# Twenty far units of a sliding-window attention backward turned by DMA instead of TensorE, with smaller K and V rings and gradient sums in four parts

## The chip, the cores and the metric

The kernel runs on one core of one Trainium2 chip. The metric is device time in microseconds (us) of one execution; several executions are timed, and one further execution is recorded by the hardware profiler. Engines are called as in the profile: PE is TensorE (PEld its weight loads), DVE is VectorE, ACT is ScalarE, POOL is GpSimd, SP is SyncE, which here only issues DMAs.

## The reference, cut to what matters

The reference is the forward and the backward of a gated mix of two branches for 2048 tokens of width 512: sliding-window attention (32 heads of 16, window 256) and a gated feed-forward network of width 1376. It returns the output and seven gradients (x, wqkv, wo, W_gate, W_up, W_down, gate_w).

```python
g = sigmoid((x * gate_w).sum(-1, keepdims=True))
a = attention(x, wqkv, wo)          # scores * Dh**-0.5, 0 <= q - k < 256, softmax
b = glu(x, W_gate, W_up, W_down)    # relu(x @ W_gate) * (x @ W_up) @ W_down
out = g * a + (1 - g) * b
_out, _vjp = jax.vjp(_f, x, wqkv, wo, W_gate, W_up, W_down, gate_w)
_grads = _vjp(grad_out)
```

## The kernel before, in words

Tokens stand in 16 tiles of 128. The program has three stages, and within each the order of all instructions is written out by hand (`tc.manual_schedule`); each engine runs its own list in that order, and semaphores make it wait for data and for free buffers.

**Stage 1 (0 to about 250 us)** is the feed-forward network: gate, up, the gradient of h, and the weight gradients (L363 to L435). **Stage 3 (from about 705 us)** computes W_down's product, wo's gradient, the output and the gradient of x (L1014 on).

**Stage 2 (about 250 to 705 us) is attention, which the change touches.** It runs over four blocks `c` of eight heads. In each block it goes over 16 query tiles `j`; each meets the key tiles `kb` = j (role "d", the diagonal), j-1 (role "m") and j-2 (role "f", far: the window's last part). Each such pair of tiles is done in two halves of four heads (`HH`), and one half is a *unit*: six units per j, from j = 2 on, in the order m, f, d (first halves) and m, d, f (second halves); 360 units in all, 112 of them far. The loop over `n` in the last part of stage 2 does, at step n:

- `front` (L687, L696 to L701) of unit n: PE's scores ST, ACT's exp into `Pu`, and on POOL the mask of d and f units;
- `front_dp` (L710) of unit n-1: PE's dPT, the product of V and the output's gradient;
- `gradp` (L715) of unit n-2: DVE's `Pd` = `Pu` * dPT;
- `rowsum` (L724, L726) of unit n-4: eight small products of PE, two for each of four heads, into BA;
- `flip`: `Pu` and `Pd` are needed with keys and queries exchanged. For d units, and for all m units but four, both halves lie in one tile (PPd, PPm; rings of three), and one DMA transpose on SP (L743), issued when the second half's `Pd` is there, turns 16 blocks of 128x128 into `p2d` or `p2m` (rings of three). The far units have tiles of their own (`Pu`, `Pd`; rings of two) and are turned on PE with rowsum: eight transposes into PSUM (`pt`, L753) and a copy by ACT or DVE (L72, L74) into a P2f tile (ring of four);
- `cd_piece` (L541, L544): for each key tile, when its last query tile is through, PE multiplies the turned tiles into CD. The pieces of one key tile stand in a list, one or two of them per step.

Beside the units there is filler work for PE, which a count (`credit`) lets in: the projections of the next group of four tiles (`project_parts`: Q, dO, a DMA transpose of both into `rows` (L181), K, V, and `tr_kv`, which writes kv with two memsets of POOL, L187 and L188), with a `due` step by which they must be in; and the sums of the gradient of wqkv of the block before (`grad_parts`, L641: four parts of four pieces of four matmuls). K and V of a group are tiles K0, K1, V0, V1, KV1, in a pool of one buffer each (pjA) and one of two (pj), so that three groups can be there. Group g+1's K and V are made while group g runs, and group g's first two query tiles still read group g-1's.

SP's list holds, in one queue, the pair transposes (L743), `rows`, the spills of finished rows to DRAM (L564, 512 KB), the stores of gradient sums (L633), and early loads of stage 3's weights: `plan` says after which group's projections a weight may be turned (`turns`, L581) or loaded (`loads`, L606, L591) into a slot that projections no longer read (x0 to x3, d0 to d3, p0 to p3); `late` spaces them out. What does not fit there (`W_rest`) is issued at the end of attention and in stage 3.

Of the kernel before, what the change touches and what calls it, by code (L numbers as in the profile page):

```python
# [11 lines left out]
BF = mybir.dt.bfloat16  # L12
# [10 lines left out]
def kernel(  # L23
# [20 lines left out]
    nc = tc.nc  # L44
    P = 128
# [9 lines left out]
    NT = S // P  # L55
# [4 lines left out]
    NTG = S // TGW  # L60
    TPG = TGW // P
# [46 lines left out]
    pjA = ctx.enter_context(tc.tile_pool(name="pjA", bufs=1))  # L108
    pjs = {}
    pools = {}  # L110

    if True:
        HH = HG // 2
# [9 lines left out]
        def project_parts(c, tg):  # L123
            t4 = {}
            proj[(c, tg)] = t4
            pj = lambda: pjA if (c * NTG + tg) % 3 == 0 else pjs["b"]

            def mm(nm, which, eng):
                ps, tag, bufs, _, _ = pools["now"]
# [68 lines left out]
    with ExitStack() as p1, tc.manual_schedule():  # L198
# [43 lines left out]
        half = TPG // 2  # L242
# [270 lines left out]
    p3 = ctx  # L513
    if True:
        st = p3.enter_context(tc.tile_pool(name="attst", bufs=2))
        gwp = p3.enter_context(tc.tile_pool(name="gwp", bufs=2))
        p3b = ExitStack()
        pjs["b"] = p3b.enter_context(tc.tile_pool(name="pj", bufs=2))
        wk = p3b.enter_context(tc.tile_pool(name="attw", bufs=2))
        pps = ExitStack()  # L520
        ps = pps.enter_context(tc.tile_pool(name="attps", bufs=2, space=PSUM))
# [61 lines left out]
        def clear(name):  # L583
            nc.gpsimd.memset(W6[(name, FC - 1)][0:FC * P - F, :], 0.0)
# [32 lines left out]
        def load_gw():  # L617
# [2 lines left out]
        plan = {2: [load_gw], 5: turns("wqkv", A_wqkv, 0, 4, "p0"), 7: turns("wqkv", A_wqkv, 4, 8, "p1"),  # L620
                11: turns("wqkv", A_wqkv, 8, 12, "p2"),
                12: turns("Wg", B_W_gate, 0, 4, "x0") + turns("Wg", B_W_gate, 4, 8, "d0"),
                15: loads("Wd", B_W_down, 0, "x3") + loads("Wd", B_W_down, 4, "d3") + loads("Wd", B_W_down, 8, "p3")}
        W_rest = (turns("Wg", B_W_gate, 8, 12, "x1") + [lambda: clear("Wg")] + turns("Wu", B_W_up, 0, 4, "d1") + turns("Wu", B_W_up, 4, 8, "x2")
                  + turns("Wu", B_W_up, 8, 12, "d2") + [lambda: clear("Wu")])

        def grad_parts(c, tail=False):
            out = []
# [33 lines left out]
        for c in range(DC):  # L662
            for j in range(NT):
                kbs = [k for k in (j - 1, j, j - 2) if k >= 0]
                for half in range(2):
                    order = kbs if half or len(kbs) < 3 else [kbs[0], kbs[2], kbs[1]]
                    for ki, kb in enumerate(order):
                        u = Unit()
                        u.c, u.j, u.kb, u.half = c, j, kb, half
                        u.first = ki == 0 and half == 0  # L670
                        u.last = ki == len(kbs) - 1 and half == 1
                        u.role = ("d", "m", "f")[j - kb]
                        u.pair = u.role == "d" or (u.role == "m" and (c < DC - 1 or j < NT - 2))
                        u.own = u.role == "f"
                        u.dma = u.pair
                        units.append(u)
        NU = len(units)

# [2 lines left out]
        def front(u):  # L681
            tg, jl = u.j // TPG, u.j % TPG
            z = zt[(u.c * NTG + tg) % ZB]
            KTt = proj[(u.c, u.kb // TPG)][f"K{u.half}"]
            ksl = slice((u.kb % TPG) * P, (u.kb % TPG + 1) * P)
            ST = ps.tile([P, HH, P], F32, tag="M", bufs=4, name="ST")
            nc.tensor.matmul(ST[:], lhsT=KTt[:, ksl], rhs=z[:, 0, :, jl, :], start=True, stop=True)  # L687
            if not u.own:
                if u.half == 0:
                    tag = f"PP{u.role}"  # L690
                    pairs[(u.c, u.j, u.kb)] = wk.tile([P, 2, 2, HH, P], BF, tag=tag, bufs=3, name=tag)
                u.PP = pairs[(u.c, u.j, u.kb)][:, u.half, :, :, :]
                u.Pu, u.Pd = u.PP[:, 0, :, :], u.PP[:, 1, :, :]
            else:
                u.Pu = wk.tile([P, HH, P], BF, tag="Pu", bufs=2, name="Pu")
            nc.scalar.activation(u.Pu[:], ST[:], ACT.Exp)  # L696
            if u.role == "d":
                nc.gpsimd.affine_select(out=u.Pu[:], in_=u.Pu[:], compare_op=ALU.is_ge, fill=0.0, base=0,  # L698
                                        pattern=[[0, HH], [1, P]], channel_multiplier=-1)
            elif u.role == "f":  # L700
                nc.gpsimd.affine_select(out=u.Pu[:], in_=u.Pu[:], compare_op=ALU.is_ge, fill=0.0, base=-1,  # L701
                                        pattern=[[0, HH], [-1, P]], channel_multiplier=1)
# [7 lines left out]
            nc.tensor.matmul(u.dPT[:], lhsT=VTt[:, ksl], rhs=z[:, 1, :, jl, :], start=True, stop=True)  # L710

        def gradp(u):
            if u.own:
                u.Pd = wk.tile([P, HH, P], BF, tag="Pd", bufs=2, name="Pd")
            nc.vector.tensor_tensor(out=u.Pd[:], in0=u.Pu[:], in1=u.dPT[:], op=ALU.mult)  # L715

        def rowsum(u):
# [17 lines left out]
        def flip(u):  # L735
            key = (u.c, u.j, u.kb, "p2")
            if u.role != "f" and key not in P2 and not (u.pair and u.half == 0):
                P2[key] = wk.tile([P, 2, 2, HH, P], BF, tag=f"P2{u.role}", bufs=3, name=f"p2{u.role}")
            if u.dma:
                if u.pair and u.half == 0:  # L740
                    return
                hs = slice(0, 2) if u.pair else slice(u.half, u.half + 1)
                nc.sync.dma_start_transpose(out=P2[key][:, hs, :, :, :].rearrange("p b a h q -> p (b a h) q"),  # L743
                                            in_=pairs[(u.c, u.j, u.kb)][:, hs, :, :, :].rearrange("p b a h q -> p (b a h q)"))
                for b in range(2)[hs]:
                    P2[(u.c, u.j, u.kb, b)] = P2[key][:, b, :, :, :]
                return
            eng = ("act", "dve", "act")[copier["i"] % 3] if u.c == 0 else ("act", "dve")[copier["i"] % 2]
            copier["i"] += 1
            pt = psr.tile([P, 2, HH, P], BF, tag="TR", name="pt")  # L750
            for a, src in enumerate((u.Pu, u.Pd)):
                for hh in range(HH):
                    nc.tensor.transpose(pt[:, a, hh, :], src[:, hh, :], ident[:])  # L753
            p2 = P2[key][:, u.half, :, :, :] if u.role == "m" else wk.tile([P, 2, HH, P], BF, tag="P2f", bufs=4, name="p2")[:]
            evac(p2, pt[:], eng)
            P2[(u.c, u.j, u.kb, u.half)] = p2

# [81 lines left out]
        with tc.manual_schedule():  # L839
# [36 lines left out]
            while n <= NU + LAG or ev or cdq or bgq:  # L876
                now = ev.pop(n, [])
                u = units[n] if n < NU else None
                if u is not None:
                    gi = u.c * NTG + u.j // TPG  # L880
                    if u.first and u.j == 0:
                        sts[u.c] = st.tile([P, NT, 4, P], BF, tag="rows_st", name="rows_st")
                    if u.first and u.j % TPG == 0:
                        if gi + 1 < len(groups):
                            prq = project_parts(*groups[gi + 1]) if gi else second
                            due = n + sum(2 * min(3, j + 1) for j in range(u.j, u.j + TPG)) - 3
                            if gi + 2 == len(groups):
                                due -= 10
                    if u.first and u.j == TPG and ends:
                        copies.append(ends.pop(0))  # L890
                    if u.first and u.j == 1 and u.c > 0:
                        ready = grad_parts(u.c - 1)
                    if u.first and u.j == TPG - 1 and u.c > 0:
                        bgq += ready
                    front(u)
                    if u.last and gi + 1 == len(groups) and u.j % TPG in (1, 3):
                        ev.setdefault(n + 2, []).append(("dma", lambda i=(u.j % TPG) // 2: load_h(i)))
# [42 lines left out]
                if n >= NU:  # L940
                    if bgq:
                        held = background()
                    elif n > NU + 1:
                        for _ in range(2):
                            if len(S2["grads"]) > DC:
                                S2["grads"].pop(0)()
                elif held and credit > 0.3:
                    held = background()
                    credit -= 0.65
                elif prq and not held and ((credit > 0.4 and n > fed + 1) or due - n <= len(prq)):  # L950
                    fed = n
                    credit -= (0.44, 0.86, 0.86, 0.1, 0.86, 0.86)[len(prq) - 1]
                    prq.pop(0)()
                    if len(prq) == 4:
                        for k in range(NP):
                            ev.setdefault(n + 1 + k, []).append(("dve", lambda gi=gi, k=k: spread(gi + 1, k)))
                        ev.setdefault(n + 1, []).append(("dma", flush))
                    if not prq:
                        late += plan.get(gi + 1, [])
                elif bgq and len(prq) <= 2 and credit > 0.3:  # L960
                    held = background()
                    credit -= 0.65
                if u is not None and u.c == DC - 1 and not bgq and u.j > 6 and "grads" not in S2:
# [177 lines left out]
```

## Time and profile before

| | us |
|---|---|
| runs shown: median (lowest, highest) | 909.66 (908.64, 911.75) |
| the profiled execution | 907.26 |
| its span on the core | 905.5 |
| PE busy | 889.5 |
| DVE, POOL, ACT busy | 511.1, 492.8, 445.5 |

The granted TensorE clock was 1.00 throughout. The costliest groups of stage 2 are ST and dPT (360 matmuls each, 136 us of modelled duration each, about 0.215 us from start to start), the exps on ACT (360 of 0.60 us), the `gradp` products on DVE (360 of 0.68 us) and the masks on POOL (240 of 0.64 us). The flips on PE are 928 transposes (116 units), with 63 copies of 1.01 us on ACT and 53 of 0.69 us on DVE; the pair transposes by DMA are 64 for d and 58 for m, of 0.5 MB each.

How to read it: a matmul's duration in the trace is that of a pipelined instruction and overlaps the next one's, so what one costs PE is read from the starts. SP's rows (SPq) are the times that SP spends on issuing a DMA, not the transfer; a transfer's end is told by its landing. "DMA share" is the mean busy share of 16 DMA engines by the sum of packet times, and can exceed 1 where packets overlap.

### The profile page before, as it was taken

The numbers are of one execution on the slowest core, as the hardware profiler recorded it, in microseconds if no ns is written. First come the engines' busy times: TensorE is split into PE (matmuls) and PEld (weight loads), VectorE is DVE, ScalarE is ACT, GpSimd is POOL, SyncE is SP. The second block draws the span as 40 slices with busy tenths as digits, with TensorE's granted clock in tenths as the row PEclk, the third lists the DMA queues.
The fourth block names the chain that finished last, engine by engine and source line by source line (L and its number), as shares of the span: only waits on it lengthen the run. The fifth ranks groups of instructions, "written<-read, shape, count | busy, mean of one in ns | idle before, by whom it ended". The sixth has DMA issues, their size and how long they took to land.

```text
span 905.5 us, 25962 instructions
## 1 busy us (share of the span) xinstructions
PE 889.5 (98%) x10607; PEld 560.2 (62%) x10607; DVE 511.1 (56%) x946; ACT 445.5 (49%) x787; POOL 492.8 (54%) x937
## 2 busy tenths in 40 slices
PE   9999999999989999999999999999999999999998
PEld 5565655655657777677776677766677544444445
DVE  4433334434368887678886788877786101333343
ACT  6422232222278778667776677766787112111111
POOL 4544545545267778767777567876787100222232
PEclk9999999999999999999999999999999999999999
DMA  9998989999799999999999989999999899998940
GB/s 301 204 193 185 198 181 210 215 216 216 180 138 159 190 185 197 185 171 156 175 187 183 184 161 183 187 193 183 192 219 190 222 243 228 275 255 218 189 134 30
DMA packets 520984, 174.57 MB, mean 193 GB/s; under 512 B 446817, under 2 KB 519745, under 8 KB 520865
## 3 DMA queue, kind: packets, MB, share of 16 engines
q1 hardware_dynamic: 498624, 150.62, 89.6%
q10 hardware_dynamic: 20608, 17.70, 7.5%
q0 software_dynamic: 1632, 4.59, 1.5%
q8 instruction: 83, 1.36, 0.6%
q14 instruction: 37, 0.30, 0.1%
HBM read 34.37 MB, written 36.24 MB: 78 GB/s over the span
## 4 chain that ended last, share of the span: by engine, by line
PE 85%; DMA 4%; DVE 4%; ACT 2%; POOL 2%; SPq 2%; issue 1%; ACTq 0%; POOLq 0%; DVEq 0%
PE dxps L1068 8%; PE wps L412 8%; PE ST L687 7%; PE dPT L710 7%; PE pt L753 5%; PE dxps L1072 4%; PE dps L414 4%; PE pp L133 4%; PE dhps L363 4%; PE ups L363 4%; PE CD L541 4%; PE gps L363 4%; PE BA L724 4%; PE wps L641 4%; PE bps L1023 3%; PE BA L726 2%
## 5 line engine op out<-in xcount | busy, mean ns | idle before, releaser
L687 PE MATMUL ST<-z,K 128*128 128x512 bf16 x360 | 135.9, 378 | 3.3 <-ACT PPd L696 1.2
L710 PE MATMUL dPT<-z,V 128*128 128x512 bf16 x360 | 136.0, 378 | 1.8 <-DVE Pd L715 0.5
L698 POOL TENSOR_SCALAR_AFFINE_SELECT PPd<-PPd 128x512 bf16<-128x512 bf16 x128 | 81.3, 636 | 80.1 <-ACT PPd L696 80.0
L377 POOL TENSOR_TENSOR hT<-rg,upm 128x512 bf16<-128x512 bf16 x44 | 51.0, 1160 | 113.8 <-DVE upm L375 97.5
L412 PE MATMUL wps<-dgu_r,x_r 128*128 128x256 bf16 (+1 forms) x704 | 103.9, 270 | 0.0
L715 DVE TENSOR_TENSOR PPd<-PPd,dPT 128x512 bf16<-128x512 bf16 x128 | 86.9, 680 | 19.9 <-PE dPT L710 12.3
L701 POOL TENSOR_SCALAR_AFFINE_SELECT Pu<-Pu 128x512 bf16<-128x512 bf16 x112 | 72.0, 643 | 35.1 <-ACT Pu L696 34.0
L696 ACT ACTIVATE PPd<-ST 128x512 bf16<-128x512 f32 x128 | 77.0, 603 | 23.6 <-PE ST L687 18.8
L715 DVE TENSOR_TENSOR Pd<-Pu,dPT 128x512 bf16<-128x512 bf16 x112 | 76.4, 682 | 21.0 <-PE dPT L710 10.6
L412 PEld LDWEIGHTS <-x_r 128*128 128x128 bf16 x704 | 68.4, 98 | 30.9 <-issue 0.2
L696 ACT ACTIVATE Pu<-ST 128x512 bf16<-128x512 f32 x112 | 67.4, 602 | 37.2 <-PE ST L687 37.1
L715 DVE TENSOR_TENSOR PPm<-PPm,dPT 128x512 bf16<-128x512 bf16 x120 | 80.1, 667 | 7.1 <-PE dPT L710 6.1
L696 ACT ACTIVATE PPm<-ST 128x512 bf16<-128x512 f32 x120 | 72.5, 604 | 16.7 <-PE ST L687 16.2
L375 DVE SCALAR_TENSOR_TENSOR upm<-rg,ups 128x512 bf16<-128x512 bf16 x44 | 30.2, 685 | 81.8 <-ACT rg L369 43.1
L369 ACT ACTIVATE rg<-gps 128x512 bf16<-128x512 f32 x44 | 26.3, 597 | 89.0 <-PE gps L363 47.4
L414 PE MATMUL dps<-db_r,h_r 128*128 128x512 bf16 x176 | 66.8, 379 | 0.0
L1048 ACT COPY a_sb<-aps 128x512 f32<-128x512 f32 x16 | 9.4, 585 | 108.0 <-issue 99.8
L72 ACT COPY p<-pt 128x1024 bf16<-128x1024 bf16 x59 | 60.1, 1019 | 4.2
L387 POOL TENSOR_TENSOR dgu<-dh_sb,rg 128x512 bf16<-128x512 bf16 x44 | 58.0, 1318 | 5.3 <-ACT dh_sb L383 5.3
L386 DVE TENSOR_TENSOR dgu<-dh_sb,upm 128x512 bf16<-128x512 bf16 x44 | 34.5, 784 | 29.8 <-ACT dh_sb L383 26.1
L641 PE MATMUL wps<-rows_st,x_r 128*128 128x384 bf16 x256 | 50.3, 325 | 0.0
L133 PE MATMUL pp<-x,p 128*128 128x512 bf16 x192 | 49.0, 378 | 0.0
(178 smaller groups left out, 2323.2 us busy)
## 6 DMA issues: line engine op xcount, KB each, us to landing
dqkvo_d<-rows_st SPq DMA_DIRECT2D x15, 512.0 KB, 4.3
hT_d<-hT ACTq DMA_DIRECT2D x44, 128.0 KB, 2.5
dgT_d<-dgu ACTq DMA_DIRECT2D x44, 128.0 KB, 2.9
duT_d<-dgu ACTq DMA_DIRECT2D x44, 128.0 KB, 3.0
h<-hT_d SPq DMA_DIRECT2D x8, 640.0 KB, 4.9
dgT_g<-dgT_d SPq DMA_DIRECT2D x8, 640.0 KB, 5.2
duT_g<-duT_d SPq DMA_DIRECT2D x8, 640.0 KB, 6.5
go_g<-in_grad_out_dram SPq DMA_DIRECT2D x16, 256.0 KB, 4.7
```

Source lines behind the costliest of these rows:

```text
L133: nc.tensor.matmul(pp[:], lhsT=w_p[c][:, cd, which * P:(which + 1) * P], rhs=x_T[tg][:, cd, :], start=(cd == 0), stop=(cd == DC - 1))
L363: nc.tensor.matmul(out[:], lhsT=w(c), rhs=x(c), start=(c == 0), stop=(c == DC - 1))
L412: nc.tensor.matmul(acc["w"][:, c, 0:2 * nw], lhsT=x_r[:, t, c * P:(c + 1) * P], rhs=k.dgu_r[:, :, i, s0:P], start=(go_ and c % 2 == 0), st ...
L414: nc.tensor.matmul(acc["d"][:], lhsT=k.h_r[:, i, :], rhs=db_r[:, t, :], start=go_, stop=no_)
L641: nc.tensor.matmul(wps[:], lhsT=x_r[:, t, part * P:(part + 1) * P], rhs=sts[c][:, t, 0:3, :], start=first and t == t0, stop=last and t == ...
L687: nc.tensor.matmul(ST[:], lhsT=KTt[:, ksl], rhs=z[:, 0, :, jl, :], start=True, stop=True)
L696: nc.scalar.activation(u.Pu[:], ST[:], ACT.Exp)
L698: nc.gpsimd.affine_select(out=u.Pu[:], in_=u.Pu[:], compare_op=ALU.is_ge, fill=0.0, base=0, pattern=[[0, HH], [1, P]], channel_multiplier=-1)
L701: nc.gpsimd.affine_select(out=u.Pu[:], in_=u.Pu[:], compare_op=ALU.is_ge, fill=0.0, base=-1, pattern=[[0, HH], [-1, P]], channel_multiplier=1)
L710: nc.tensor.matmul(u.dPT[:], lhsT=VTt[:, ksl], rhs=z[:, 1, :, jl, :], start=True, stop=True)
L715: nc.vector.tensor_tensor(out=u.Pd[:], in0=u.Pu[:], in1=u.dPT[:], op=ALU.mult)
L1068: nc.tensor.matmul(to, lhsT=src[:, fc, lsl], rhs=W6[(wt, fc)][:, cols], start=(fc == 0 and wt == "Wg"), stop=False)
```

## The change

- In blocks 1, 2 and 3, 20 far units of the first half (j = 3, 4, 5, 6, 8, 9, 10, without 10 in block 3) are flipped by a DMA transpose of their own (eight blocks of 128x128), issued on SP three steps after the unit's front, instead of by PE.
- Every far unit has one tile for `Pu` and `Pd`: PFa (first halves, ring of three) or PFb (second halves, ring of one). P2f's ring grows from four to five.
- The pool pj has one buffer instead of two, and groups alternate between pjA and pj: K and V stand in rings of two. A `gate` holds back the K projection (and with it V and kv) until step 12 of the group (5 in a block's first group), when the older group's buffers come free; `due` of the last group is 6 instead of 10 steps early.
- The gradient sums of the block before are released in four parts, at j = 3, 5, 9 and 13, instead of all at j = 3, and may also run while the K projection waits at its gate.
- W_down is loaded into x1, d1 and x2 after groups 13 and 14 (it was x3, d3, p3 after group 15), and the weights of `W_rest` go into d2, x3, d3, p3.

```diff
--- before.py
+++ after.py
@@ -123,7 +123,7 @@
         def project_parts(c, tg):
             t4 = {}
             proj[(c, tg)] = t4
-            pj = lambda: pjA if (c * NTG + tg) % 3 == 0 else pjs["b"]
+            pj = lambda: pjA if (c * NTG + tg) % 2 == 0 else pjs["b"]
 
             def mm(nm, which, eng):
                 ps, tag, bufs, _, _ = pools["now"]
@@ -515,7 +515,7 @@
         st = p3.enter_context(tc.tile_pool(name="attst", bufs=2))
         gwp = p3.enter_context(tc.tile_pool(name="gwp", bufs=2))
         p3b = ExitStack()
-        pjs["b"] = p3b.enter_context(tc.tile_pool(name="pj", bufs=2))
+        pjs["b"] = p3b.enter_context(tc.tile_pool(name="pj", bufs=1))
         wk = p3b.enter_context(tc.tile_pool(name="attw", bufs=2))
         pps = ExitStack()
         ps = pps.enter_context(tc.tile_pool(name="attps", bufs=2, space=PSUM))
@@ -620,9 +620,9 @@
         plan = {2: [load_gw], 5: turns("wqkv", A_wqkv, 0, 4, "p0"), 7: turns("wqkv", A_wqkv, 4, 8, "p1"),
                 11: turns("wqkv", A_wqkv, 8, 12, "p2"),
                 12: turns("Wg", B_W_gate, 0, 4, "x0") + turns("Wg", B_W_gate, 4, 8, "d0"),
-                15: loads("Wd", B_W_down, 0, "x3") + loads("Wd", B_W_down, 4, "d3") + loads("Wd", B_W_down, 8, "p3")}
-        W_rest = (turns("Wg", B_W_gate, 8, 12, "x1") + [lambda: clear("Wg")] + turns("Wu", B_W_up, 0, 4, "d1") + turns("Wu", B_W_up, 4, 8, "x2")
-                  + turns("Wu", B_W_up, 8, 12, "d2") + [lambda: clear("Wu")])
+                13: loads("Wd", B_W_down, 0, "x1") + loads("Wd", B_W_down, 4, "d1"), 14: loads("Wd", B_W_down, 8, "x2")}
+        W_rest = (turns("Wg", B_W_gate, 8, 12, "d2") + [lambda: clear("Wg")] + turns("Wu", B_W_up, 0, 4, "x3") + turns("Wu", B_W_up, 4, 8, "d3")
+                  + turns("Wu", B_W_up, 8, 12, "p3") + [lambda: clear("Wu")])
 
         def grad_parts(c, tail=False):
             out = []
@@ -672,7 +672,7 @@
                         u.role = ("d", "m", "f")[j - kb]
                         u.pair = u.role == "d" or (u.role == "m" and (c < DC - 1 or j < NT - 2))
                         u.own = u.role == "f"
-                        u.dma = u.pair
+                        u.dma = u.pair or (u.own and half == 0 and j in ((), (3, 4, 5, 6, 8, 9, 10), (3, 4, 5, 6, 8, 9, 10), (3, 4, 5, 6, 8, 9))[c])
                         units.append(u)
         NU = len(units)
 
@@ -692,7 +692,9 @@
                 u.PP = pairs[(u.c, u.j, u.kb)][:, u.half, :, :, :]
                 u.Pu, u.Pd = u.PP[:, 0, :, :], u.PP[:, 1, :, :]
             else:
-                u.Pu = wk.tile([P, HH, P], BF, tag="Pu", bufs=2, name="Pu")
+                tag, bufs = (("PFa", 3), ("PFb", 1))[u.half]
+                u.PP = wk.tile([P, 2, HH, P], BF, tag=tag, bufs=bufs, name=tag)
+                u.Pu, u.Pd = u.PP[:, 0, :, :], u.PP[:, 1, :, :]
             nc.scalar.activation(u.Pu[:], ST[:], ACT.Exp)
             if u.role == "d":
                 nc.gpsimd.affine_select(out=u.Pu[:], in_=u.Pu[:], compare_op=ALU.is_ge, fill=0.0, base=0,
@@ -710,8 +712,6 @@
             nc.tensor.matmul(u.dPT[:], lhsT=VTt[:, ksl], rhs=z[:, 1, :, jl, :], start=True, stop=True)
 
         def gradp(u):
-            if u.own:
-                u.Pd = wk.tile([P, HH, P], BF, tag="Pd", bufs=2, name="Pd")
             nc.vector.tensor_tensor(out=u.Pd[:], in0=u.Pu[:], in1=u.dPT[:], op=ALU.mult)
 
         def rowsum(u):
@@ -736,6 +736,12 @@
             key = (u.c, u.j, u.kb, "p2")
             if u.role != "f" and key not in P2 and not (u.pair and u.half == 0):
                 P2[key] = wk.tile([P, 2, 2, HH, P], BF, tag=f"P2{u.role}", bufs=3, name=f"p2{u.role}")
+            if u.dma and u.own:
+                p2 = wk.tile([P, 2, HH, P], BF, tag="P2f", bufs=5, name="p2f")
+                nc.sync.dma_start_transpose(out=p2[:].rearrange("p a h q -> p (a h) q"),
+                                            in_=u.PP[:].rearrange("p a h q -> p (a h q)"))
+                P2[(u.c, u.j, u.kb, u.half)] = p2[:]
+                return
             if u.dma:
                 if u.pair and u.half == 0:
                     return
@@ -751,7 +757,7 @@
             for a, src in enumerate((u.Pu, u.Pd)):
                 for hh in range(HH):
                     nc.tensor.transpose(pt[:, a, hh, :], src[:, hh, :], ident[:])
-            p2 = P2[key][:, u.half, :, :, :] if u.role == "m" else wk.tile([P, 2, HH, P], BF, tag="P2f", bufs=4, name="p2")[:]
+            p2 = P2[key][:, u.half, :, :, :] if u.role == "m" else wk.tile([P, 2, HH, P], BF, tag="P2f", bufs=5, name="p2")[:]
             evac(p2, pt[:], eng)
             P2[(u.c, u.j, u.kb, u.half)] = p2
 
@@ -885,13 +891,15 @@
                             prq = project_parts(*groups[gi + 1]) if gi else second
                             due = n + sum(2 * min(3, j + 1) for j in range(u.j, u.j + TPG)) - 3
                             if gi + 2 == len(groups):
-                                due -= 10
+                                due -= 6
+                            gate = n + (12 if u.j else 5)
                     if u.first and u.j == TPG and ends:
                         copies.append(ends.pop(0))
                     if u.first and u.j == 1 and u.c > 0:
                         ready = grad_parts(u.c - 1)
-                    if u.first and u.j == TPG - 1 and u.c > 0:
-                        bgq += ready
+                    if u.first and u.c > 0 and u.j in (3, 5, 9, 13):
+                        bgq += ready[:NT // 4]
+                        del ready[:NT // 4]
                     front(u)
                     if u.last and gi + 1 == len(groups) and u.j % TPG in (1, 3):
                         ev.setdefault(n + 2, []).append(("dma", lambda i=(u.j % TPG) // 2: load_h(i)))
@@ -947,7 +955,7 @@
                 elif held and credit > 0.3:
                     held = background()
                     credit -= 0.65
-                elif prq and not held and ((credit > 0.4 and n > fed + 1) or due - n <= len(prq)):
+                elif prq and not held and (len(prq) > 3 or n >= gate) and ((credit > 0.4 and n > fed + 1) or due - n <= len(prq)):
                     fed = n
                     credit -= (0.44, 0.86, 0.86, 0.1, 0.86, 0.86)[len(prq) - 1]
                     prq.pop(0)()
@@ -957,7 +965,7 @@
                         ev.setdefault(n + 1, []).append(("dma", flush))
                     if not prq:
                         late += plan.get(gi + 1, [])
-                elif bgq and len(prq) <= 2 and credit > 0.3:
+                elif bgq and (len(prq) <= 2 or len(prq) == 3 and n < gate) and credit > 0.3:
                     held = background()
                     credit -= 0.65
                 if u is not None and u.c == DC - 1 and not bgq and u.j > 6 and "grads" not in S2:
```

## Prediction

> **What bounds the kernel now.** I read the engine table and the slices first, then the windows by attention block, then SP's timeline, then ACT's waits at the end of attention.
>
> ```profile
> span 905.5 us, 25962 instructions
> PE 889.5 (98%) x10607; PEld 560.2 (62%) x10607; DVE 511.1 (56%) x946; ACT 445.5 (49%) x787; POOL 492.8 (54%) x937
> ...
> q1 hardware_dynamic: 498624, 150.62, 89.6%
> ```
>
> PE has 16 us of idle time in all. Matmul ends are modelled, so I also went by starts: 512 columns hold PE 0.215 us, a 128x128 transpose 0.055, a BA or CD matmul 0.025. The blocks (8 heads each) run 251 to 358, 474, 590 and 700 us; columns are PE, PEld, DVE, ACT, POOL busy, clock, DMA share, GB/s:
>
> ```profile
> 358.00:474.00 116.00, 115.53 (x2022) 81.37 (x2019) 89.78 (x169) 83.68 (x151) 84.87 (x196) 1.00 1.09 176
> 474.00:590.00 116.00, 115.14 (x2009) 80.93 (x2007) 90.57 (x170) 83.22 (x149) 84.79 (x196) 1.00 1.07 181
> 590.00:700.00 110.00, 106.77 (x1915) 76.27 (x1913) 82.55 (x152) 78.65 (x140) 81.06 (x188) 1.00 1.12 194
> ```
>
> PE sets the pace; DVE, the next engine, has 22% to spare. But the DMA share is above 1 (packets overlap), and SP's queue shows what that means (start, duration):
>
> ```profile
> 449.31 1.24 SPq L181 DMA_TRANSPOSE rows<-zT  x1
> 450.66 3.00 SPq L743 DMA_TRANSPOSE p2m<-PPm  x1
> 453.76 2.38 SPq L743 DMA_TRANSPOSE p2d<-PPd  x1
> 456.25 2.11 SPq L743 DMA_TRANSPOSE p2m<-PPm  x1
> 458.46 3.72 SPq L743 DMA_TRANSPOSE p2d<-PPd  x1
> 462.28 1.65 SPq L743 DMA_TRANSPOSE p2m<-PPm  x1
> 464.06 3.71 SPq L743 DMA_TRANSPOSE p2d<-PPd  x1
> 467.95 1.81 SPq L743 DMA_TRANSPOSE p2m<-PPm  x1
> 470.25 3.48 SPq L743 DMA_TRANSPOSE p2d<-PPd  x1
> 473.79 0.57 SPq L564 DMA_DIRECT2D dqkvo_d<-rows_st  x1
> ```
>
> Each transposing DMA starts some 0.1 us after the one before: the queue is full. Here a query tile j needs two pair transposes, 5.8 us, and PE needs 5.86 us for the same j (6 ST, 6 dPT, 48 BA, 48 CD, 16 transposes). Two resources are level. That lateness costs is seen once (waits of ACT, 660 to 700 us):
>
> ```profile
> ACT PPd L696 <- DMA p2d<-PPd: 2.2, 1, 2.2
> ```
>
> An exp waits for a PPd buffer whose transpose is still under way; PE loses 2.4 us between 683 and 690, after the W_down loads (L606, 666 to 669) were put into that queue.
>
> **The change, part by part.**
>
> *Taken from PE:* 20 flips of 8 transposes. From the first transpose of one flip (300.63) to the dPT behind it (301.08) is 0.45 us: 20 x 0.45 = 9.0 us, 6.3 in blocks 1 and 2 (7 units each), 2.7 in block 3. The instruction order has 160 transposes fewer on PE, 10 evacuations fewer on ACT (1.01 us each) and 10 on DVE (0.69); those two are off the path and count nothing.
>
> *Put on SP:* 20 DMA transposes of 128x1024. The trace has that very shape, rows<-zT: 1.28 us on the queue (1.23 to 1.96), 3.3 us to land. I take 1.3. They go ahead of their tile's two pairs and delay them by as much. Their readers (CD, L541) come 10 units later, about 12 us.
>
> *Spreading:* by the order, PE work per j in block 1 goes from 9.35, 8.88, 8.66, 9.31, 6.95, 7.58, 8.02, 5.86 (j = 3 to 10) to 7.61, 7.14, 8.01, 7.58, 5.86, 7.14, 8.01, 7.58; j = 13 gets 8.45. The sum falls by the flips alone. What it buys is that a j with a far DMA lasts 7.1 us or more.
>
> *K and V in rings of two:* the K projection waits for the 12th unit of its group, V and kv follow. POOL's memset of kv (L187) now waits for a BA matmul; behind it in POOL's queue is the next mask, whose exp comes later on PE anyway. Cost 0; if that cover fails, one BA wait of 0.4 us (as at L724) in 15 groups, 6 us; an earlier memset can't gain, for kv was never late. In block 0 the first K projection moves about 2 units, among start-up gaps of PE of 0.3 to 0.7 us: -0.9 to +0.9 (its own length), taken as 0. The single PFb buffer is free 2 units before its next exp: 0; at worst one 0.6 us exp late.
>
> *W_down earlier:* 1.4 MB leave the tail (j > 9) for j = 5 to 7 of block 3. The tail's 2.4 us should mostly go (j = 13 also has 2.6 us more PE work): -1.5, between -2.4 and 0.
>
> **The sum that decides: SP's queue.** Prices with the gap: pair 2.83 (medians 2.57 for p2d, 2.89 for p2m), far or rows 1.3, weight turn 1.75 (L581: 1.3 to 2.5), spill 1.4 and store 0.7 (their issue, and for the spill what its 512 KB take), W_down 4.5 in all (the four issues take 3.3 us; from 660 to 678 the lag of p2m, from the pair's last gradp to its issue, grew from 0.1 to 6). Checked on before, block 3, the p2m of j = 3 to that of j = 9: 12 pairs, 3 turns, 2 rows, 2 spills, 4 stores = 47.4 us, against 48.5 measured.
>
> How much lag is free? PPm is written again 12 us after it is ready at 6 us per j (312.58 to 324.54), so about 14.5 at 7.3; landing takes 5.3. A lag over some 9 us stops ACT, then PE. A far unit: 12.8 - 3.3, about the same.
>
> Blocks 1 and 2, p2m of j = 3 to that of j = 11: 16 pairs, 6 far, 2 turns, 2 rows, 2 spills, 2 stores = 63.4, against 58.1 of PE. The lag rises by 5.3 from 1.4 (block 1) or 3.4 (block 2), with a hump near 8 at j = 8. Just inside; the 6.3 us are kept.
>
> Block 3, j = 3 to j = 10: 14 pairs (39.6), 5 far (6.5), 4 turns (7.0), 2 rows (2.6), 2 spills (2.8), 3 stores (2.1), W_down (4.5) = 65.1, against 51.6 of PE; the lag at j = 3 was 5.3, and one turn that stood ahead of it is gone while one far unit is added: 4.9. So 4.9 + 65.1 - 51.6 = 18.4, and 9 are free: PE waits some 9 us. With pairs at 2.73, without the gap, it is 8. I take 7.5, since lags on the way into block 3 measured about 1 us under this sum; ends 3 and 14.
>
> -6.3 - 2.7 + 7.5 - 1.5 = **-3.0 us**. The profiled execution took 907.26 (span 905.5 and 1.8 around it), the median of the runs shown is 909.66, 2.4 more. 907.26 - 3.0 = 904.3, and in the median's terms **906.7**.
>
> Against bytes: block 3 moved 194 x 110 = 21.3 MB; with 6 x 0.26 MB more and one turn less, 22.7 MB in 105.8 us would be 214 GB/s. No 25 us window of attention shows over 205.
>
> **Rivals.**
>
> *The queue has room* (A). Then PE pays all: -9.0 - 1.5, 899.2. For it: the fastest pair took 1.65 us, so two pairs and a far unit could take 4.6 us of a 7.1 us j. Against: pairs average 2.8 whenever the queue is full. The Trainium skill (DMA: Bandwidth & Descriptors, Latency and other measured facts) gives DMA transposes 350 to 400 GB/s, 261 in one kernel; an estimate by that page is 1.4 us for a pair's 0.5 MB, so A would follow. The trace disagrees: eight pairs in 23 us are 182 GB/s. Chance 0.22.
>
> *The queue is the bound in blocks 1 and 2 too* (C, the other side). It decides where a pair costs over 2.9 or a far unit over 1.4 in a full queue: 16 pairs at 2.93 add 1.6 to the lag and 6 far units at 1.6 add 1.8, so block 1 passes the free lag, block 2 starts later still, and block 3 waits 12 to 14. Then some 3 to 5 us of waits go into blocks 1 and 2: -6.3 - 2.7 + 4 + 13 - 1 = +7, 916.7. For it: 18.6 us for 6 pairs and a rows (2.9 per pair). Against: block 3 of before, the one long backlog, fits 2.7 to 2.8. The Trainium skill (VectorE: DVE Perf Modes, The three transpose paths) speaks against the change too: 390 ns for a 128x128 transpose on TensorE, 1309 by DMA, TensorE where PSUM will do. By that page a far unit would be 10.5 us, an estimate; the row of 3.3 us to land says less. Chance 0.2.
>
> *Nothing gained, nothing lost* (D): far DMAs land after their CD already in blocks 1 and 2 because each stands behind the previous j's pairs; PE waits as long as it saved: 909.7 to 911. Chance 0.13.
>
> That the flips stay on PE is excluded by the instruction order.
>
> **Chances.** Forecast 0.45, A 0.22, C 0.2, D 0.13. This kernel's measurement tells some 0.3% (2.7 us) from no change. The forecast's own spread (stall 3 to 12) is 902 to 911: 0.45 splits into 0.24 faster, 0.19 the same, 0.02 slower. Faster: 0.24 + 0.22 = 0.46. Same: 0.19 + 0.10 of D = 0.29. Slower: 0.02 + 0.03 + 0.2 = 0.25. Range: 899.5 (A) to 915 (most of C).
>
> **What would show it.** Right: PE's transposes (pt) 160 fewer; SP back to back from j = 3 to 10 in blocks 1 to 3; blocks 1 and 2 shorter by about 3 us each; block 3 no shorter, with PE's CD (L541) or ACT's exp waiting for p2f, p2m or p2d; no such wait near 688. Wrong: block 3 shorter by 3 or more (A); waits for p2f in block 1 (C, D); p2f taking clearly other than 1.3 us on the queue; PE waits at the K or V projections or POOL's memset.

## The result, and the profile after

The changed kernel takes 924.22 us (median of five runs, 922.19 to 927.86); the kernel before, on the same chip, 909.42 (908.64 to 911.75). The ratio is 1.0161, 95% interval 1.0143 to 1.018: slower by 15 us, where 3 us less had been forecast. The profiled execution of the changed kernel is the longest of the five, 927.86 us, and that of before, 907.26, lies under the lowest of its runs; so the two traces differ by 20.6 us where the medians differ by 14.8.

The page of the changed kernel, span, engines and SP's DMA queue:

```profile
span 926.1 us, 25629 instructions
PE 891.9 (96%) x10447; PEld 555.3 (60%) x10447; DVE 497.7 (54%) x936; ACT 434.0 (47%) x777; POOL 492.0 (53%) x937
...
q1 hardware_dynamic: 519744, 155.86, 91.5%
```

PE has 160 instructions fewer, as the change says; 20 x 0.26 MB more go through the queue. Yet PE is idle for 34 us where it was idle for 16. The windows by block (columns: PE, PEld, DVE, ACT, POOL busy, clock, DMA share, GB/s) show where:

```profile
355.50:470.60 115.10, 112.97 (x1958) 78.08 (x1954) 84.98 (x164) 79.41 (x146) 83.94 (x196) 1.00 1.20 191
470.60:589.20 118.60, 114.28 (x1952) 78.60 (x1949) 86.44 (x166) 78.97 (x146) 85.17 (x198) 0.99 1.16 187
589.20:719.00 129.80, 114.91 (x1937) 78.03 (x1934) 82.61 (x153) 79.35 (x143) 83.69 (x195) 0.95 1.10 193
```

Block 3 lasts 129.8 us and PE works in 114.9 of them, with a granted clock of 0.95 on average. The GB/s of block 3 stayed where they were (193 for 194 before): there the queue moves no more per us, it moves longer. In blocks 1 and 2 they rose, from 176 and 181 to 191 and 187. PE's waits and the far tiles' DMA (min/median/max: ns on SP's queue, us from issue to landing):

```profile
PE CD L541 <- DMA p2f<-PFa: 15.2, 12, 3.4
PE CD L541 <- DMA p2m<-PPm: 4.0, 5, 1.4
```

```profile
L741 SPq DMA_TRANSPOSE p2f<-PFa x20: 1242/1617/2367, 378.9 to 681.6; - x20
...
DMA to landing us min/median/max: 3.2/4.9/5.8
```

From here on a block is measured from PE's first ST of it to the first ST of the next (block 3: to the last ST). In these stretches the comparison is free of what the loads of stages 1 and 3 add from run to run. Where no far DMA stands they repeat to 0.1 us between kernels that run the same instructions (block 0 takes 103.9 us in the nine kernels with the smaller rings). With far DMAs they repeat less well: the same blocks 1 and 2 took 115.0 and 118.7 us here, 115.2 and 117.8 in e2 below, 115.3 and 118.0 in e6. So the block times of this trace, the longest run, are somewhat over those of the median run. From the starts of the matmuls, each stretch splits into work at full clock, waits, and what a lower granted clock adds:

| | block 0 | block 1 | block 2 | block 3 |
|---|---|---|---|---|
| before: us | 101.9 | 115.5 | 115.9 | 114.6 |
| after: us | 103.9 | 115.0 | 118.7 | 129.8 |
| work, before / after | 96.2 / 96.2 | 112.9 / 109.8 | 112.9 / 109.8 | 109.1 / 106.4 |
| waits, before / after | 5.7 / 7.8 | 2.6 / 5.2 | 3.0 / 7.5 | 5.5 / 19.4 |
| lower clock, before / after | 0.0 / 0.0 | 0.0 / 0.0 | 0.0 / 1.3 | 0.0 / 4.0 |

One far unit shows the waiting. DVE finishes its product (start, duration) at 625.43 in the timeline of DVE:

```profile
624.74 0.69 DVE L715 TENSOR_TENSOR PFa<-PFa,dPT 128x512 bf16<-128x512 bf16 x1 [0.24 <-PE dPT L712]
```

Its DMA starts at 645.04 on SP's queue, 19.6 us later, behind ten others that stand back to back:

```profile
626.40 3.05 SPq L749 DMA_TRANSPOSE p2d<-PPd  x1
629.51 1.29 SPq L581 DMA_TRANSPOSE x<-in_B_W_gate_dram  x1
630.91 0.58 SPq L633 DMA_DIRECT2D out_dram<-ws  x1
631.53 0.62 SPq L564 DMA_DIRECT2D dqkvo_d<-rows_st  x1
632.25 1.82 SPq L741 DMA_TRANSPOSE p2f<-PFa  x1
634.17 1.46 SPq L181 DMA_TRANSPOSE rows<-zT  x1
635.69 1.44 SPq L581 DMA_TRANSPOSE d<-in_B_W_gate_dram  x1
637.23 3.30 SPq L749 DMA_TRANSPOSE p2m<-PPm  x1
640.63 2.97 SPq L749 DMA_TRANSPOSE p2d<-PPd  x1
643.65 1.29 SPq L581 DMA_TRANSPOSE d<-in_B_W_gate_dram  x1
645.04 1.64 SPq L741 DMA_TRANSPOSE p2f<-PFa  x1
```

And PE, with nothing else in its list ahead of that CD, stands still until it lands:

```profile
648.75 0.21 PE L541 MATMUL CD<-rq,p2f 128*128 128x32 bf16 x1 [3.39 <-DMA p2f<-PFa]
```

### The profile page after: what moved, and what is told of

It reads as the page before. It is cut to its first block, busy times and chain, and to the rows that moved or that the text cites. A ratio compares the mean times of both kernels' runs of the same rounds, so it can differ in the third digit from the quotient of the medians.

```text
span 926.1 us, 25629 instructions
## 1 busy us (share of the span) xinstructions
PE 891.9 (96%) x10447; PEld 555.3 (60%) x10447; DVE 497.7 (54%) x936; ACT 434.0 (47%) x777; POOL 492.0 (53%) x937
## 5 line engine op out<-in xcount | busy, mean ns | idle before, releaser
L700 POOL TENSOR_SCALAR_AFFINE_SELECT PPd<-PPd 128x512 bf16<-128x512 bf16 x128 | 81.7, 639 | 115.5 <-ACT PPd L698 115.4
L412 PE MATMUL wps<-dgu_r,x_r 128*128 128x256 bf16 (+1 forms) x704 | 103.9, 270 | 0.4 <-DVE wst L74 0.3
L412 PEld LDWEIGHTS <-x_r 128*128 128x128 bf16 x704 | 68.4, 98 | 31.7 <-issue 1.2
L72 ACT COPY p<-pt 128x1024 bf16<-128x1024 bf16 x49 | 50.3, 1027 | 1.4
L363 PE MATMUL gps<-x,Wg_sb 128*128 128x512 bf16 x176 | 46.0, 384 | 0.3 <-DVE x L74 0.3
L703 POOL TENSOR_SCALAR_AFFINE_SELECT PFa<-PFa 128x512 bf16<-128x512 bf16 x56 | 37.1, 662 | 16.8 <-ACT PFa L698 16.6
L698 ACT ACTIVATE PFa<-ST 128x512 bf16<-128x512 f32 x56 | 33.6, 600 | 26.0 <-PE ST L687 25.9
```

The lines of the kernel that those rows point to most:

```text
L72: nc.scalar.copy(out, in_)
L412: nc.tensor.matmul(acc["w"][:, c, 0:2 * nw], lhsT=x_r[:, t, c * P:(c + 1) * P], rhs=k.dgu_r[:, :, i, s0:P], start=(go_ and c % 2 == 0), st ...
```

## The experiments

Theory (called Q in the expectations): SP's queue is overfilled by the far DMAs, and PE's CD waits for what comes late. Rivals: the smaller K and V rings cost the time (K), or the earlier W_down loads do (W). Each ratio is to the kernel before on the same chip.

| kernel | median us | ratio, 95% interval | blocks 0 to 3, us |
|---|---|---|---|
| e1: no far DMA, rest of the change | 911.47 | 1.0021 (1.0007 to 1.0035) | 103.9, 115.6, 116.0, 114.3 |
| e2: far DMAs in blocks 1 and 2 | 915.13 | 1.0058 (1.0038 to 1.0079) | 103.9, 115.2, 117.8, 118.7 |
| e3: far DMAs in block 3 | 920.49 | 1.0113 (1.009 to 1.0137) | 103.9, 115.6, 116.0, 124.4 |
| e4: far units not turned | 906.21 | 0.996 (0.9946 to 0.9974) | 103.9, 113.2, 113.2, 115.0 |
| e5: before + K, V rings | 912.3 | 1.0033 (1.0019 to 1.0047) | 103.9, 117.4, 117.8, 115.0 |
| e6: change, W_down late | 920.86 | 1.0121 (1.0093 to 1.0149) | 103.9, 115.3, 118.0, 123.7 |
| e7: far DMAs on ACT's queue | 996.84 | 1.0972 (1.0945 to 1.0999) | 103.9, 144.0, 142.4, 146.3 |
| e8: before + 7 far DMAs | 910.32 | 1.0014 (0.9999 to 1.0028) | 102.3, 114.1, 114.9, 114.2 |
| e9: before + gradients in four | 907.88 | 0.9981 (0.9971 to 0.9992) | 101.9, 115.0, 115.4, 114.5 |
| e10: e4, W_down late | 906.5 | 0.9969 (0.9955 to 0.9983) | 103.9, 113.3, 113.2, 114.1 |
| e11: e8, W_down early | 912.55 | 1.0039 (1.0026 to 1.0052) | 102.3, 114.1, 114.9, 114.9 |
| e12: e9 + 6 far DMAs | 907.15 | 0.9971 (0.9958 to 0.9985) | 102.3, 114.8, 114.5, 115.6 |

**e1, e2, e3: the far DMAs, and where.** One line is edited, the list of the far DMAs (e1 shown; e2 empties the last tuple, e3 the two before it):

```diff
-u.dma = u.pair or (u.own and half == 0 and j in ((), (3, 4, 5, 6, 8, 9, 10), (3, 4, 5, 6, 8, 9, 10), (3, 4, 5, 6, 8, 9))[c])
+u.dma = u.pair or (u.own and half == 0 and j in ((), (), (), ())[c])
```

> All 20 far units go back to TensorE transposes, and the rest of the change stays (K and V in rings of two, gradient sums in four parts, W_down earlier). Theory Q (SP's transposing queue is overfilled by the far DMAs, CD waits for p2f and p2m, above all in block 3, and after the waits TensorE runs some 4 us at a lower clock): the waits of CD in blocks 1 to 3 (4.5, 2.5 and 16.1 us) and the low clock go, the 9.0 us of flips come back, and 908 to 911 us remain; block 3 falls from 129.8 us to 113 to 116, and the 2 us that block 0 gained stay. Rival K (the rings of two and their gate cost the time): 915 us or more, with waits at the K and V projections in all blocks. Rival W (the W_down loads in block 3 are what overfills the queue): about 915 us, block 3 still over 120.

> The far DMAs stay in blocks 1 and 2 (14 units) and block 3 goes back to TensorE transposes. Theory Q: block 3 falls to 113 to 117 us and blocks 1 and 2 stay at 115.0 and 118.7 us, 911 to 914 us in all. Rival K: over 916 us. Rival W: 918 us or more, block 3 over 120.

> The far DMAs stay in block 3 alone (6 units). Theory Q: blocks 1 and 2 at about 115 to 116 us, block 3 still 122 to 128 (its start is some 3 us less late than after two filled blocks), 917 to 921 us in all. Rival K: as after, 922 to 925 us, for the far units are not what costs. Rival W: about 923 us, since W_down is there as before.

All three came out as theory Q has them, e1 0.5 and e2 1.1 us over its range (block 3 of e2 took 118.7 us for 113 to 117), e3 in it. Without far DMAs 12.8 of the 15 us go (924.22 to 911.47). The far units of blocks 1 and 2 cost 3.7 us over e1, those of block 3 9.0, and the two add up to the whole. In e2 block 3 has no far unit and still takes 118.7 us for 114.3: it begins with the queue late. PE's waits for turned tiles in block 3, first of e1, then of e2, then of e3:

```profile
PE CD L541 <- DMA p2m<-PPm: 0.9, 1, 0.9
```

```profile
PE CD L541 <- DMA p2m<-PPm: 4.0, 4, 1.7
```

```profile
PE CD L541 <- DMA p2m<-PPm: 5.4, 4, 1.6
PE CD L541 <- DMA p2f<-PFa: 4.7, 4, 2.3
```

A backlog that far DMAs leave in block 2 is paid by the pairs (p2m) of block 3. W falls as the main cause: W_down was loaded early in e1 too, and its block 3 took 114.3 us.

**e4, e10: TensorE's saving without the queue's cost.** e4 leaves the turning of the 20 far tiles out of the computation: CD reads the unturned tile.

```diff
             if u.dma and u.own:
-                p2 = wk.tile([P, 2, HH, P], BF, tag="P2f", bufs=5, name="p2f")
-                nc.sync.dma_start_transpose(out=p2[:].rearrange("p a h q -> p (a h) q"),
-                                            in_=u.PP[:].rearrange("p a h q -> p (a h q)"))
-                P2[(u.c, u.j, u.kb, u.half)] = p2[:]
+                P2[(u.c, u.j, u.kb, u.half)] = u.PP
                 return
```

> The turning of 20 far tiles is left out altogether: CD reads the unturned tile, with neither TensorE transposes nor DMAs. This is TensorE's saving without the queue's cost. Theory Q: 9.0 us under the kernel with the far units on TensorE, 899 to 902 us. Rival K: 912 us or more. Rival W: some 905 us, with waits of CD for p2m in block 3.

A miss that tells much: 5.3 us under e1, not 9.0. Blocks 1 and 2 fall by 2.4 and 2.8 us of the 3.15 that left PE; block 3 falls by nothing (115.0 for 114.3). There SP's queue holds the time even when the far units cost it nothing: by the starts, of the 2.7 us that left PE 2.0 came back as waits, and 1.4 more as a stretch at half the granted clock behind the longest of them. PE waits for a pair (waits of PE in block 3),

```profile
PE CD L541 <- DMA p2m<-PPm: 2.8, 2, 2.5
```

so the 2.7 us of flips in block 3 were not to be won without making room in that queue. e10 puts the W_down loads back to see whether they are what fills it.

> The kernel that leaves out the turning of the 20 far tiles, with the W_down loads put back to where they were. Theory Q: with the loads in block 3 SP's queue is level with TensorE there even without a far DMA, which is why block 3 kept 115.0 us when 2.7 us of TensorE's work were taken out of it. Without the loads it should fall to 112 to 113 us; the wait near its end may return with 1 to 2 of that: 904 to 906 us. Rival: block 3 is held by something else than the queue, and stays at 114.5 to 115.5 us: 906 to 907 us.

In between: block 3 at 114.1, 0.9 less, and the whole the same. The loads are only part of it. ACT's exps in block 3 of e10 still wait for pair tiles whose transposes are under way:

```profile
ACT PPd L698 <- DMA p2d<-PPd: 2.9, 2, 2.3
ACT PPm L698 <- DMA p2m<-PPm: 1.3, 2, 1.0
```

**e6: the W_down loads beside the far DMAs.** `plan` and `W_rest` as before the change.

```diff
-13: loads("Wd", B_W_down, 0, "x1") + loads("Wd", B_W_down, 4, "d1"), 14: loads("Wd", B_W_down, 8, "x2")}
+15: loads("Wd", B_W_down, 0, "x3") + loads("Wd", B_W_down, 4, "d3") + loads("Wd", B_W_down, 8, "p3")}
```

> The changed kernel with the W_down loads and the order of the weight turns put back to where they were (plan 15). Theory Q, with no free lag left in block 3, so that each us taken from SP's queue there is a us of time: the W_down loads were 4.5 us of it, so block 3 falls from 129.8 to 124 to 126 us, and the wait near its end returns with up to 2.4: 919 to 922 us. Rival (only the transposes count, the W_down loads fit between them): block 3 within 1.5 us of 129.8, 923 to 926 us.

As theory Q has it: block 3 falls by 6.1 us to 123.7 (the medians differ by 3.4; the trace of the changed kernel is that of its longest run). The two other pairs of kernels that differ in these loads alone have them early at 0.7 us (block 3 of e11 against e8 below) and 0.9 us (e4 against e10). What an item in the queue costs is decided by the backlog it meets.

**e5, e9: the rings and the gradient sums alone.** e5 takes the edits of `pj`, its pool, `due` and `gate` into the kernel before; e9 only this:

```diff
-                    if u.first and u.j == TPG - 1 and u.c > 0:
-                        bgq += ready
+                    if u.first and u.c > 0 and u.j in (3, 5, 9, 13):
+                        bgq += ready[:NT // 4]
+                        del ready[:NT // 4]
```

> The kernel before with the rings of two for K and V alone (with their gate in the planner). It is to tell where the 2 us come from that the kernel with all far units on TensorE is slower than before, and that block 0 lost in every run (103.9 for 101.9 us) although no far DMA is in it. If the rings are the cause: block 0 at 103.9 us, blocks 1 to 3 as before within 0.5 us, 910.5 to 912 us. Rival: the spread gradients or the earlier W_down cost it, and the rings nothing: block 0 at 101.9, 909 to 910 us.

> The kernel before with the gradient sums in four parts alone. The rings of two for K and V alone lengthened blocks 1 and 2 by 1.9 us each, and with the spread gradients beside them the blocks stood at 115.6 and 116.0, as before. Theory: the spread sums only fill the places where the late K and V leave TensorE idle; alone they find 2.6 to 2.7 us of waits per block and change blocks 1 to 3 by less than 1 us: 908.5 to 910.5 us. Rival: they are worth some 2 us per block by themselves: 113.7 us a block, 903 to 906 us.

The rings cost 2.0 us in block 0, as expected, and 1.9 in each of blocks 1 and 2, which was not: 6.2 us in all four by the blocks, 3.2 by the medians; why the two differ is open, the trace of e5 being that of its longest run. PE's ST waits for DVE's products (waits of PE, whole span; before had 1.2, 2, 0.6):

```profile
PE ST L687 <- DVE PPm L715: 4.7, 8, 0.6
```

In blocks 1 and 2 PE stands still for 0.7 and 0.2 us early in j = 9 and again in j = 13, while the gate holds K back and no gradient sum is left to fill the time. The spread sums fill it in e1, whose blocks 1 and 2 take what they took before. Alone (e9) the sums are worth 0.5 us in each of blocks 1 and 2, and the median is 0.19% under before, a little under the range given. So the change's +2.1 us without its far DMAs is block 0, where there are no sums to fill with.

**e7: another queue.** `nc.sync.dma_start_transpose` of the far unit becomes `nc.scalar.dma_start_transpose`.

> The changed kernel with the 20 far DMAs issued on ScalarE's queue instead of SP's. If it is the order in SP's queue that costs (the far unit stands ahead of its pairs and behind those of the tile before): p2f lands in some 3.3 us, the waits of CD for p2f go, and with each us of queue worth a us of time 908 to 914 us. Rival: the 16 DMA engines behind the queue are what is full, so the same bytes take the same time from any queue: 920 to 926 us, with the pairs on SP taking longer than 2.8 us while a far unit runs.

Neither: it was not the test it was meant to be. In the built program each of these DMAs stands on ACT behind waits for the transposes then under way on SP's queue. p2f lands in 3.1 us and no CD waits for it, but the exps behind it wait (the trace puts 32.1 us of it, in five waits, down to the landing of p2d), and PE for them (timeline of ACT, then waits of PE):

```profile
392.81 1.26 ACTq L741 DMA_TRANSPOSE p2f<-PFa  x1
394.12 0.60 ACT L698 ACTIVATE PFb<-ST 128x512 bf16<-128x512 f32 x1 [3.98 <-issue]
```

```profile
PE dPT L712 <- ACT PFb L698: 48.9, 14, 6.8
```

Whether two queues together would move more than one stays open.

**e8, e11, e12: a version that wins?** e8 puts seven far DMAs into the kernel before (j = 3 to 6 of block 1, 3 to 5 of block 2), with PFa in a ring of two and only KV1 in a ring of two; e11 adds the early W_down; e12 is e8 with the spread sums and this list:

```diff
+u.dma = u.pair or (u.own and half == 0 and j in ((), (3, 5, 9), (3, 5, 9), ())[c])
```

> The kernel before with seven far DMAs only where the queue's lag was lowest in the trace (j = 3 to 6 of block 1, j = 3 to 5 of block 2), far tiles in rings of two and one, K and V in rings of three as before with only the small KV tile in a ring of two, W_down and gradient sums as before. Theory Q: the flips' 7 x 0.45 = 3.2 us are kept, since 7 x 1.6 us of queue fit where PE needs 8.5 to 9 us for a j: 905.5 to 907 us, blocks 1 and 2 shorter by 1.8 and 1.4 us, block 0 101.9 us. Rival (a far DMA never pays, each costs its 1.6 us later in the same block): 909 to 914 us, with waits of CD at j = 7 to 11.

> The kernel with seven far DMAs in the roomy places of blocks 1 and 2, and with the early W_down loads of the changed kernel. With late loads its attention was 2.4 us shorter than before, but what follows attention took 214 us for 207 to 208 in all the others, after a store on ScalarE's queue that took 4.35 us to issue. If that is the late loads' doing (they were late in the kernel before as well), this one keeps the 2.4 us: 906 to 907.5 us. Rival: it was that one execution or the kernel's own end, and it stays at 909 to 911 us.

> The spread gradient sums (alone 1.5 us under before) with six far DMAs put where a tile of TensorE's work is longest with them (j = 3, 5, 9 of blocks 1 and 2, 8.4, 10.3 and 10.3 us, for some 7.3 us of queue), the small KV tile in a ring of two, W_down as before. Theory Q: far DMAs in places with over 1.6 us of room keep their 0.45 us each: blocks 1 and 2 at 113.7 and 114.1 us with no wait of CD for p2f, 905 to 907 us; with the wait of 3 to 4 us that both kernels with seven far DMAs met after attention, 908 to 910 us. Rival (no far DMA pays): blocks 1 and 2 at 115 us or more, 908 to 911 us.

In e8 blocks 1 and 2 are shorter by 1.4 and 1.0 us (1.8 and 1.4 were expected), without a wait for p2f: where the lag is small, a far DMA pays there. But the kernel is not faster (910.32 for 905.5 to 907). After attention, ACT's first store of the last sums (L633) takes 4.35 us to issue, beside two weight turns on SP, and PE waits for the copy behind it; the same line of before, then of e8, then e8's wait:

```profile
L633 ACTq DMA_DIRECT2D out_dram<-ws x4: 542/564/650, 715.7 to 718.7; - x4
```

```profile
L633 ACTq DMA_DIRECT2D out_dram<-ws x4: 541/563/4352, 713.6 to 720.3; - x4
```

```profile
PE dwo L1034 <- ACT ws L72: 3.8, 1, 3.8
```

e11 meets the same (3.83 us, a wait of 2.6) and takes 912.55 us, over both its ranges, so the late loads are not the cause; that it is the store's place among SP's turns was not tried. In e12 it is absent (0.77 at most), no CD waits for p2f, and it is the fastest kernel here that leaves nothing out, 0.29% under before. Against e9 its gain is small: blocks 1 and 2 take 114.8 and 114.5 for 115.0 and 115.4 (113.7 and 114.1 were expected), block 3, which has no far DMA, 1.1 more, and the two intervals overlap.

## Why the prediction was wrong, by its own steps

**The step that failed** is the one that set the free lag against the queue: "The lag rises by 5.3 from 1.4 (block 1) or 3.4 (block 2), with a hump near 8 at j = 8. Just inside; the 6.3 us are kept", and in block 3 "the lag at j = 3 was 5.3, and one turn that stood ahead of it is gone while one far unit is added: 4.9". The start lags were those of before, and the change raises them from block to block; and the hump, taken to lie inside the free lag at j = 8, came to 12.2 at j = 5 of block 2.

- *Block 2* began the stretch with 6.5 us of lag (3.4 taken), since block 1 handed on more; the far unit of j = 5 was 12.2 us late, and PE waited. 6.3 us were to be kept in blocks 1 and 2; the blocks show -0.5 and +2.8.
- *Block 3.* The lag of p2m at j = 3 was 10.4, not 4.9. From the two traces: the block starts with 2.1 us more in the queue although the turn is gone (so blocks 1 and 2 hand on about 4), five pairs take 1.6 longer, a far unit 1.2. The queue from j = 3 to 10 took 67.4 us for 65.1 worked out. Put into the same sum: 10.4 + 67.4 - 51.6 = 26.2, of which 9.8 were left as lag at j = 10: 16.4 us of stretching for the 9 of the prediction. The start value makes 5.5 of the difference, the queue's work 2.3, and the free lag, 9.8 for 9, takes 0.8 off. (That PE's stretch was 67.9 for 51.6, 16.3 more, follows from how lag is defined and confirms nothing by itself; by the starts it is 52.7 of work, 12.5 of waits, against 2.2 in e1, and 2.7 of lower clock.)
- *The sum stopped at j = 10.* From j = 11 to 15 block 3 lost another 6.2 us (37.9 for 31.7 of work), while the lag came down from 9.8 at j = 10 to 3.5 at j = 13. e1 loses 1.5 there, so 4.7 are the backlog's.
- *Far unit.* 1.3 us on the queue and 3.3 to land were taken from a queue that was not full; in it they were 1.62 and 4.9 (medians). In e12, with room, 1.35 and 4.4. So the free lag of some far units was less than the 9 taken: in blocks 1 and 2 PE waited for units that were 6.2, 7.0 and 7.6 us late as well as for those at 9.2 and more, though not for others at up to 8.9.
- *K and V rings: 0.* Wrong: 6.2 us by the blocks of e5, 3.2 by the medians; 6 had been given for the cover failing, but in blocks 1 and 2 it is ST that waits, not BA. The spread sums give back what blocks 1 and 2 lose.
- *W_down: -1.5.* No gain: moving it earlier made block 3 longer by 0.7 (e11 against e8) and 0.9 (e4 against e10), and with the backlog of the far DMAs by 6.1 (the changed kernel against e6; 3.4 by the medians).
- *Flips: 9.0.* Right for PE's work (3.1, 3.1 and 2.7 in the table); but with the queue's cost taken out altogether it is worth 5.3 us of time (e4; 4.4 by the blocks).

Rival C named the mechanism, the queue as the bound in blocks 1 and 2 too, with "block 2 starts later still"; it put block 3's waits at 12 to 14 and those of blocks 1 and 2 at 3 to 5; measured, by the table, they grew by 13.9 and 7.1. It was held too unlikely because block 3 of before fitted pairs of 2.7 to 2.8 us. C's condition (a pair over 2.9 or a far unit over 1.4 in a full queue) was met: from j = 3 to 10 of block 3, from start to start on SP's queue, the 14 pairs took 3.23 us each and the five far units 1.54; from j = 3 to 11 of blocks 1 and 2 the pairs took 2.88 and 2.73, the far units 1.63 and 1.93. In block 3 the pairs alone took 5.7 us more than the prediction's price; turns, spills and W_down took 4.7 less, which hid it in the sum.

The page of the Trainium skill cited there (VectorE: DVE Perf Modes, The three transpose paths), which gives a 128x128 transpose 390 ns on TensorE and 1309 by DMA, had the direction right for the 20 units as they are placed here; the six of e12 cost PE no wait.

Of what was to be seen, 160 pt fewer, SP back to back (467 to 623 us without a gap over 0.25 us) and CD waiting for p2f in block 3 were there. The wait near 688 did not go: PE waits there for p2f and p2m, 1.4 and 1.2 us, now for tiles of an earlier j. And the waits for p2f in block 1 (1.3 us) were the sign given for C and D.

## What to carry to other kernels

Before work is moved to a queue that is level with the bounding engine, follow its lag from one block to the next and look at the peak: what a stage hands on costs the stage after it, and the same transfer held up no CD where there was room (six in e12) and cost 1.5 us where the queue was behind (six in e3: 9.0 us). When an engine is relieved, take its work out of the kernel first (as e4 does): it shows what there is to gain, here 5.3 of 9.0 us, and that in one of three blocks there is nothing. Of a bundle of edits, run the ones that look neutral alone, too.

## What the runs showed of the hardware

A wait of PE costs more than its length. Three stretches of 3.41 us in the changed kernel, one after the other (first column after the stretch: its length; PE busy; the clock is the seventh number):

```profile
519.94:523.35 3.41, 1.43 (x33) 0.94 (x32) 1.97 (x4) 0.84 (x2) 3.11 (x8) 1.00 0.95 188
523.35:526.77 3.42, 3.42 (x46) 2.30 (x43) 1.15 (x3) 2.86 (x5) 0.05 (x1) 0.50 1.04 200
526.77:530.18 3.41, 3.41 (x60) 2.33 (x57) 1.93 (x4) 1.29 (x3) 2.88 (x7) 1.00 1.29 135
```

In the first PE waits for 2.1 us in one piece and is idle for 2.3 by its starts; in the next the granted clock is half, and 512 columns take 0.427 us for 0.215. The halved stretches of this trace begin at 523.4, 636.0, 646.2 and 697.4, whole multiples of 3.413 us apart. In attention, each of the five such stretches that follow idle time of about 1.6 us or more in the one before is halved, and none that follows 1.4 or less. In other traces the border is less sharp: 1.47 was followed by a halved stretch in e2, and 1.59, at the start of attention, was not in e4. The Trainium skill (TensorE: Matmul & The Clock Gate, Part 1) has a free-running window of about 3.4 us and a throttle after an idle window; here a window that was idle for about half was enough. In block 3 this added 4.0 us to PE's work. How much of that is time is not settled: while PE waits for the queue anyway, a slower PE only waits less.

The queue's time is not all its own work. The page of the changed kernel counts 81 fetches of instructions of 16 KB each (queue q8); 46 of them begin in blocks 1 to 3. By the packet records, the queue's packets, some 75 to 80 done per 0.1 us ahead of such a fetch, fall to about 5 from 0.8 to 1.6 us after its start: a near stop of 1.35 us (median), about 60 us over the 363 us of the three blocks. The kernel before shows the same (47 fetches, 1.35 us). So this is part of what a pair costs in both kernels, and not of the difference between them; that the fetch is the cause is read from the fixed distance and was not tried.
